# Output products in alternating row halves from one pool of six banks, turned weights for sixteen places at once, and softmaxes split into steps two pairs ahead

## The chip, the cores and the metric

One NeuronCore of a Trainium2 chip runs the whole program. The metric is the device time of one execution in microseconds (us); lower is better. The engines named below are PE (TensorE, matrix products), DVE (VectorE), ACT (ScalarE), POOL (GpSimd) and SP (SyncE, which issues the DMAs here). SBUF is the on-chip memory, PSUM the eight accumulator banks that PE writes and that DVE and ACT empty, HBM the memory outside.

## The reference

`x` is 8 x 2496 x 256, in fp32. Two Fourier transforms are followed by a soft mixture of experts with 32 slots:

```python
X = np.fft.fft(np.fft.fft(x, axis=1), axis=2).real      # 8 x 2496 x 256, seen as N x 256
logits = X @ phi                                        # N x 32
d = softmax(logits, over the N rows)                    # dispatch
slot_in = d.T @ X                                       # 32 x 256
slot_out = relu(slot_in @ w1[e]) @ w2[e]                # 8 experts, 4 slots each
c = softmax(logits, over the 32 slots)                  # combine
out = c @ slot_out                                      # N x 256
```

Every max is subtracted before its exponential and 1e-9 is added to each sum. The output is 20.45 MB of fp32.

## The kernel before, in words

The eight sequences are handled as four pairs p = 0 to 3. The table `ORDER` writes out the parts of the program in order, one letter for a part, one digit for the pair, one for a piece of it. A scheduler then puts the instructions of all parts into one queue for each engine; each engine runs its queue strictly in order, and `tc.issue_after(x)` keeps what it encloses behind the instruction x in that order.

**The first part** (parts a, z, t, b, c, e, d, u) loads x, folds and transforms it, makes logits (tile `lt`, kept for each pair), and accumulates the dispatch sums. It ends with the last sums of pair 3 (`u`, L376). **The middle** takes up about 20 us: `m` joins the pairs' sums (`accT`, `slotin`, and the slot inputs `sT`, L455 to L457), `l` is the first expert product (`h`, L475, then a ReLU on ACT into `hs`, L483, and a transpose on DVE into `hT`, L487), `v` the second (`so`, L495), and `r` replicates the slot outputs: `so` is copied to `sos` (L509 on ACT, L510 on DVE), multiplied with a selection matrix (`sorep`, L511), and scaled into the two halves of the operand `rh` (L512 on ACT, L513 on DVE).

**The softmax over slots** is part `s`, once for each pair: eleven transposes of `lt` into three PSUM banks (`cT`, L525), three copies on ACT into `c` (L530), and then, for each of two halves of 20 places, a max on DVE (L539), a subtraction on POOL (L540), the exponential on ACT (L541), a sum, an addition and a reciprocal on DVE (L542 to L544) and a multiplication on POOL (L545). Pairs 0 and 1 get theirs in the middle of the program, pairs 2 and 3 within the output stage; all stand behind the last `u` product.

**The output stage** is part `o`, for each pair five blocks b = 0 to 4 of eight places. For a block, PE transposes two 128-column pieces of `c` (`lT`, L555), ACT copies them to SBUF (`lTs`, L558), and four products `po` follow (L565), i = 0 to 3. Each product uses only 64 of the array's 128 rows: i = 0 and 2 use rows 0 to 63, i = 1 and 3 use rows 64 to 127 (`tile_position=(64 * (i % 2), 0)`). Each fills one PSUM bank (128 x 512). The even products take their bank from a pool of two (`ps`), the odd ones from a pool of three (`ps3`), and a seventh and eighth bank (`p1`) hold transposes. ACT copies the even products into the output tile `o` (128 x 2048, 1 MB), DVE the odd ones (L579). When a tile is full, SP issues its DMA to HBM (L586, and L584 for a 128 KB rest of each pair). The output tiles come from a ring of six buffers that x and the weights used before.

Every fp32 product appears in the trace as two records, each transpose as one.

Of the kernel before, what the change touches and what calls it, by code (L numbers as in the profile page):

```python
# [114 lines left out]
def _build(nc, tc, xh, phih, w1h, w2h, cins, where, out, out0):  # L115
# [4 lines left out]
    with ctx:  # L120
        cp = ctx.enter_context(tc.tile_pool(name="cp", bufs=1))
        sb = ctx.enter_context(tc.tile_pool(name="sb", bufs=1))
        pp = ctx.enter_context(tc.tile_pool(name="pp", bufs=P2, space=PSUM))
# [303 lines left out]
        def part_m():  # L427
# [21 lines left out]
            pe.matmul(ps[:1, 64:96], acc[:, 0:1], C("psum")[:, 0:32], start=True, stop=True)  # L449
            v.tensor_copy(at[:, :64], ps[:, :64])  # L450
            v.tensor_copy(at[:1, 32:64], ps[:1, 64:96])
            for lc in range(2):
                ps = bank3(f"slotin{lc}")
                ls = slice(lc * 128, lc * 128 + 128)
                pe.matmul(ps[:, :NSLOT], C("ta")[:, ls], at[:, 0:32], start=True, stop=False)  # L455
                pe.matmul(ps[:, :NSLOT], C("tb")[:, ls], at[:, 32:64], start=False, stop=True)
                (sc.copy, v.tensor_copy)[lc](sT[:, lc], ps[:, :NSLOT])  # L457
# [45 lines left out]
        def part_r():  # L503
# [5 lines left out]
            sc.copy(sos[:, :128], so[:, :128])  # L509
            v.tensor_copy(sos[:, 128:], so[:, 128:D])  # L510
            pe.matmul(ps[:, :D], C("sel2"), sos, start=True, stop=True)  # L511
            sc.activation(rh[0][:, 0], ps[:, :D], AF.Copy, scale=C("turn")[:, 0:1])  # L512
            v.tensor_scalar(rh[0][:, 1], ps[:, :D], C("turn")[:, 1:2], None, op0=ALU.mult)  # L513


        cq = {}

        def part_s(p):
            L = lt[p]
            cq[p] = sb.tile([128, 40, NSLOT], F32, name=f"c{p}", tag=CT[p], bufs=bufs_(CT[p]))  # L520
            for b in range(3):
                ps = bank1(f"cT{p}_{b}")
                n = min(4, NG - 4 * b)
                for j in range(n):
                    pe.transpose(  # L525
                        ps[:, 120 * j : 120 * j + 120],
                        L[:, 4 * b + j].rearrange("p s k -> p (s k)"), ident[:120, :120],
                    )
# [5 lines left out]
            e1 = nc.gpsimd if GP & 1 else v  # L534
            e2 = nc.gpsimd if GP & 2 else v
            for i in range(2):
                c = cq[p][:, 20 * i : 20 * i + 20]
                m = sb.tile([128, 2, 20], F32, name=f"cm{p}_{i}", tag="cm", bufs=2)
                v.tensor_reduce(m[:, 0], c, axis=AX.X, op=ALU.max)  # L539
                e1.tensor_tensor(c, c, m[:, 0].unsqueeze(2).to_broadcast([128, 20, NSLOT]), op=ALU.subtract)  # L540
                sc.activation(c, c, AF.Exp)  # L541
                v.tensor_reduce(m[:, 1], c, axis=AX.X, op=ALU.add)  # L542
                v.tensor_scalar(m[:, 1], m[:, 1], 1e-9, None, op0=ALU.add)
                v.reciprocal(m[:, 1], m[:, 1])  # L544
                e2.tensor_tensor(c, c, m[:, 1].unsqueeze(2).to_broadcast([128, 20, NSLOT]), op=ALU.mult)  # L545


        n_ev = [0]

        def part_o(p, b):  # L550
            ps = bank1(f"lT{p}_{b}")
            lT = et([128, 2, 128], f"lTs{p}_{b}")
            for t in range(2):
                k0 = 8 * b + 4 * t
                pe.transpose(  # L555
                    ps[:, t * 128 : t * 128 + 128], cq[p][:, k0 : k0 + 4].rearrange("p k s -> p (k s)"), ident
                )
            sc.copy(lT, ps[:, :256].rearrange("p (i n) -> p i n", i=2))  # L558
            ot = ring(f"o{p}_{b}")

            pos = []
            for i in range(4):
                pos.append((bank, bank3)[i % 2](f"po{p}_{b}_{i}"))
                rows = slice(64 * (i % 2), 64 * (i % 2) + 64)
                pe.matmul(  # L565
                    pos[i], lT[rows, i // 2], rh[0][rows].rearrange("p k d -> p (k d)"),
                    start=True, stop=True, tile_position=(64 * (i % 2), 0),
                )
                if i % 2 == 0:
                    continue  # L570
                part_ev(p, b, i - 1, pos[i - 1], ot)
                part_ev(p, b, i, pos[i], ot)

        done_ = {}

        def part_ev(p, b, i, po, ot):
            done = done_.get((p, b), 0)
            np_ = 64 if b == 4 and i == 3 else 128
            (v.tensor_copy if n_ev[0] % 2 else sc.copy)(  # L579
                ot[:np_, 2 * i : 2 * i + 2, :].rearrange("p k d -> p (k d)"), po[:np_]  # L580
            )
            n_ev[0] += 1
            if b == 4 and i == 3:
                nc.sync.dma_start(out0[p].rearrange("p (r d) -> p r d", d=D), ot[:64, 6:8])  # L584
            elif i == 3 or (b == 4 and i == 2) or ((p, b) == (0, 0) and i in FIRST):
                nc.sync.dma_start(  # L586
                    out[p, :, (8 * b + done) * D : (8 * b + 2 * i + 2) * D].rearrange("p (r d) -> p r d", d=D),
                    ot[:, done : 2 * i + 2],
                )
                done_[p, b] = 2 * i + 2  # L590
# [66 lines left out]
```

## Time and profile before

| | |
|---|---|
| time, median of 3 runs | 203.47 us (203.37 to 204.8) |
| the profiled execution: device time | 203.76 us |
| the profiled execution: span of the trace | 201.7 us |
| granted PE clock over the span | 0.982 |
| moved to and from HBM | 38.46 MB read, 20.45 MB written |

The device time of the profiled execution holds 2.06 us that lie outside the span. It is 0.29 us above the median. Times inside the trace count from the start of the span.

### The profile page before, as it was taken

How to read it: one execution, taken by the hardware profiler on the slowest of the kernel's cores; microseconds unless marked ns; L12 is line 12 of the kernel's file. 1: busy time of each engine (PE TensorE's matmuls, PEld its weight loads, DVE VectorE, ACT ScalarE, POOL GpSimd, SP SyncE). 2: the span in 40 equal slices, each digit the busy share in tenths (PEclk: the TensorE clock that was granted, in tenths of full speed). 3: DMA queues.
4: the chain of work that ended last, by engine and by line, in shares of the span. 5: the costliest groups of instructions: out<-in, count | busy, mean ns of one | idle time of the engine just before them, and what ended most of it. 6: DMA issues, size and time to landing. Idle time of an engine off the chain costs nothing.

```text
span 201.7 us, 4216 instructions
## 1 busy us (share of the span) xinstructions
PE 178.7 (89%) x1682; PEld 110.1 (55%) x1682; DVE 126.0 (62%) x228; ACT 111.9 (55%) x252; POOL 20.8 (10%) x25
## 2 busy tenths in 40 slices
PE   0489899899999899999989999997998999999930
PEld 0365586586778766568738772564443343334400
DVE  0599869999968926422575448634668458465600
ACT  2134686578872864757628355534657456556630
POOL 0000000000000000000000025730016225200000
PEclk9999999999999999999999999999999999999975
DMA  5999999999930998009506799801978588599996
GB/s 181 412 422 412 416 421 424 418 419 411 353 138 10 354 406 369 5 0 305 219 3 240 292 310 414 318 0 41 368 289 336 245 362 329 219 418 387 422 382 265
DMA packets 10706, 59.16 MB, mean 293 GB/s; under 512 B 1344, under 2 KB 1728, under 8 KB 5696
## 3 DMA queue, kind: packets, MB, share of 16 engines
q1 hardware_dynamic: 10688, 58.91, 73.9%
q8 instruction: 13, 0.21, 0.4%
q14 instruction: 5, 0.04, 0.0%
HBM read 38.46 MB, written 20.45 MB: 292 GB/s over the span
## 4 chain that ended last, share of the span: by engine, by line
PE 80%; DVE 6%; ACT 5%; DMA 2%; issue 1%; POOL 1%; SPq 0%; ACTq 0%; DVEq 0%
PE po L565 22%; PE pt L229 9%; PE z L244 8%; PE e L335 6%; PE d L353 5%; PE a L279 4%; PE u L376 4%; PE h L475 4%; PE so L495 3%; PE lT L555 3%; DMA x<-xh 2%; PE cT L525 2%; PE lp L297 2%; PE lm L298 2%; PE zt L265 2%; ACT et L230 2%
## 5 line engine op out<-in xcount | busy, mean ns | idle before, releaser
L565 PE MATMUL po<-rh,lTs 64*128 64x512 f32 x160 | 47.6, 617 | 1.7 <-DVE rh L513 1.1
L579 DVE COPY o<-po 128x512 f32<-128x512 f32 (+1 forms) x40 | 27.3, 686 | 14.8 <-PE po L565 14.6
L579 ACT COPY o<-po 128x512 f32<-128x512 f32 x40 | 23.4, 587 | 19.8 <-PE po L565 19.6
L229 PE MATMUL pt<-cs,eo 128*128 128x128 f32 x160 | 25.7, 294 | 8.2 <-DVE eo L224 7.9
L230 ACT COPY et<-pt 128x512 f32<-128x512 f32 x40 | 22.8, 587 | 14.3 <-PE pt L229 14.2
L565 PEld LDWEIGHTS po<-rh,lTs 64*128 64x128 f32 x160 | 17.9, 185 | 19.1 <-issue 8.8
L229 PEld LDWEIGHTS pt<-cs,eo 128*128 128x128 f32 x160 | 19.1, 149 | 14.8 <-DVE eo L224 7.9
L222 DVE TENSOR_TENSOR x<-x 128x1024 f32<-128x1024 f32 x16 | 19.4, 1215 | 3.2 <-DMA x<-xh 3.2
L244 PE MATMUL z<-et,wphi 128*32 128x256 f32 (+1 forms) x288 | 16.7, 368 | 2.3 <-ACT et L230 2.3
L540 POOL TENSOR_TENSOR c<-c,cm 128x640 f32<-128x640 f32 x8 | 10.0, 1265 | 74.8 <-DVE cm L539 73.6
L320 ACT ACTIVATE d<-lt,nm 120x128 f32<-120x128 f32 x44 | 13.7, 391 | 3.6 <-DVE nm L317 3.6
L335 PE MATMUL e<-cs,dpm 120*64 120x120 f32 x176 | 13.9, 273 | 0.0
L224 DVE TENSOR_TENSOR eo<-x 128x512 f32<-128x512 f32 x20 | 13.6, 682 | 0.3
L225 DVE TENSOR_TENSOR eo<-x 128x512 f32<-128x512 f32 x20 | 13.6, 680 | 0.0
L244 PEld LDWEIGHTS z<-et,wphi 128*32 128x32 f32 x288 | 8.1, 114 | 9.2 <-ACT et L230 3.8
L279 PE MATMUL a<-cs,zt 128*120 128x128 f32 x88 | 11.8, 279 | 1.0 <-DVE lt L302 0.9
L335 PEld LDWEIGHTS e<-cs,dpm 120*64 120x64 f32 x176 | 11.4, 136 | 2.4 <-issue 1.8
L252 ACT COPY zs<-z 128x512 f32<-128x512 f32 (+1 forms) x12 | 6.2, 513 | 10.4 <-PE z L244 10.4
L376 PE MATMUL u<-eo,ds 128*32 128x129 f32 x320 | 11.5, 275 | 0.1
L279 PEld LDWEIGHTS a<-cs,zt 128*120 128x120 f32 x88 | 10.4, 183 | 2.1 <-DVE lt L302 1.1
L353 PE MATMUL d<-e,cs 128*64 128x320 f32 x64 | 10.7, 443 | 0.5 <-ACT ds L359 0.5
L545 POOL TENSOR_TENSOR c<-c,cm 128x640 f32<-128x640 f32 x8 | 10.1, 1264 | 6.6 <-DVE cm L544 6.6
(94 smaller groups left out, 219.2 us busy)
## 6 DMA issues: line engine op xcount, KB each, us to landing
x<-xh SPq DMA_DIRECT2D x16, 1024.0 KB, 12.0
out<-o SPq DMA_DIRECT2D x15, 1024.0 KB, 4.3
w<-w1h SPq DMA_DIRECT2D x6, 1024.0 KB, 8.0
w<-w2h SPq DMA_DIRECT2D x12, 512.0 KB, 6.5
x<-xh SPq DMA_DIRECT2D x4, 896.0 KB, 12.4
out<-o SPq DMA_DIRECT2D x4, 768.0 KB, 4.3
w<-w1h SPq DMA_DIRECT2D x4, 512.0 KB, 5.5
w<-w2h SPq DMA_DIRECT2D x2, 1024.0 KB, 7.2
```

Source lines behind the costliest of these rows:

```text
L222: v.tensor_tensor(x[:, 0:4], x[:, 0:4], x[:, 4:8], op=ALU.add)
L224: v.tensor_tensor(e[:, :, 0:128], x[:, 0:4, 0:128], x[:, 0:4, 128:256], op=ALU.add)
L229: pe.transpose(b[:, g * 128 : g * 128 + 128], e[:, g, k * 128 : k * 128 + 128], ident)
L230: sc.copy(tr[k][:, :, :, qi, :], b.rearrange("p (g h a) -> p g h a", g=4, h=2))
L244: pe.matmul(z[32 * g : 32 * g + 32, o : o + n], wphi[:, w, :], tr[k][:, g].rearrange("p h q a -> p (h q a)"), start=w != 0, stop=w != 1, t ...
L279: pe.matmul(ps[:120, i * 128 : i * 128 + 128], zt[p][:, GS * g : GS * g + GS].rearrange("p s h c -> p (s h c)"), C("wa"), start=True, stop ...
L320: sc.activation(d[:, g], L[:, g], AF.Exp, bias=nm[:, g : g + 1], scale=1.0)
L335: pe.matmul(ps[64 * k : 64 * k + 64, 120 * i : 120 * i + 120], dpm[p, hf][:, k, 3 * j + i, :], C(name), start=True, stop=True, tile_positi ...
L353: pe.matmul(ps[64 * h : 64 * h + 64, :320], C("wb")[:, 64 * k : 64 * k + 64], esb[p].rearrange("p g (s h c) -> p (g s) h c", h=2, c=NKC)[: ...
L376: last = pe.matmul(ub[32 * g : 32 * g + 32, 0:129], dsb[p][:, k, c, :], e[:, 0:129] if k == 0 else e[:, 127:256], start=cc == 0, stop=cc == 9,
L565: pe.matmul(pos[i], lT[rows, i // 2], rh[0][rows].rearrange("p k d -> p (k d)"), start=True, stop=True, tile_position=(64 * (i % 2), 0),)
L579: (v.tensor_copy if n_ev[0] % 2 else sc.copy)(ot[:np_, 2 * i : 2 * i + 2, :].rearrange("p k d -> p (k d)"), po[:np_])
```

## The change

The products of a block are written in couples: two banks are taken from one pool `po` of six banks, product h = 0 (rows 0 to 63) and h = 1 (rows 64 to 127) are queued one behind the other, and each product is held behind the one before it. ACT empties h = 0, DVE h = 1. The six banks are those of the old pools `ps`, `ps3` and `u`, which are closed after part `r`.

The transposes of `c` move into a part of their own, `k`, with sixteen places at a time for j = 0 and 1 and eight for j = 2: four, four and two transposes, and one copy on ACT for each (128x512, 128x512, 128x256).

The softmaxes of pairs 2 and 3 become six steps, part `x`: transposes and copies; both maxima and subtractions; one exponential; the other; sum to multiplication of one half; of the other. `ORDER` puts the steps of pair 2 between the blocks of pair 0, and those of pair 3 between blocks of pairs 1 and 2. Parts `k` and `x` are held behind the latest product and the latest copies of `o`.

In the middle, the transposes of pairs 0 and 1 are held behind `u`, `accT` or `slotin` one by one (`GATE`), the rest of their softmaxes behind the copies of `sT`, and both of those copies are made by DVE. `sos` is one copy on ACT, and both halves of `rh` are made on ACT.

```diff
-    "u30 m00 l00 s00 l10 s10 v00 v10 r00 o00 o01 o02 o03 "
-    "o04 o10 s20 o11 o12 o13 o14 s30 o20 o21 o22 o23 "
+    "u30 m00 l00 s00 l10 s10 v00 v10 r00 k00 o00 k01 x20 o01 x21 o02 k02 x22 o03 "
+    "k10 x23 o04 x24 o10 k11 x25 o11 x30 o12 k12 x31 o13 k20 x32 o14 x33 o20 k21 "
...
+GATE = {0: ['u', 'acc', 'acc'], 1: ['slot', 'slot', 'slot']}
...
-                (sc.copy, v.tensor_copy)[lc](sT[:, lc], ps[:, :NSLOT])
+                anchor["sT"] = v.tensor_copy(sT[:, lc], ps[:, :NSLOT]).ins
...
-            sc.copy(sos[:, :128], so[:, :128])
-            v.tensor_copy(sos[:, 128:], so[:, 128:D])
+            sc.copy(sos, so[:, :D])
...
-            v.tensor_scalar(rh[0][:, 1], ps[:, :D], C("turn")[:, 1:2], None, op0=ALU.mult)
+            for k in range(2):
+                sc.activation(rh[0][:, k], ps[:, :D], AF.Copy, scale=C("turn")[:, k : k + 1])
+            banks.close()
+            pool_o.append(ctx.enter_context(tc.tile_pool(name="po", bufs=6, space=PSUM)))
...
+        def part_s(p):
+            logits(p)
+            with tc.issue_after(anchor["sT"]):
+                for i in range(2):
+                    less_max(p, i)
+                    exp(p, i)
+                    over_sum(p, i)
...
+            n = 4 if j < 2 else 2
+            lT = et([128, 4, 128], f"lTs{p}_{j}")
...
+            sc.copy(lT[:, :n], ps[:, : 128 * n].rearrange("p (i n) -> p i n", i=n))
...
+                po = [pool_o[0].tile([128, 512], F32, name=f"po{p}_{b}_{2 * t + h}", tag="po") for h in range(2)]
+                for h in range(2):
+                    rows = slice(64 * h, 64 * h + 64)
+                    with tc.issue_after(behind["pe"]) if "pe" in behind else nullcontext():
+                        ins = pe.matmul(
+                            po[h], lts[p, b, t][rows], rh[0][rows].rearrange("p k d -> p (k d)"),
+                            start=True, stop=True, tile_position=(64 * h, 0),
+                        )
+                    behind["pe"] = ins.ins
+                for h, ev in ((0, sc.copy), (1, v.tensor_copy)):
+                    i = 2 * t + h
...
+                    behind[h] = ins.ins
...
+                for ins in behind.values() if behind else [anchor["u"]]:
+                    order.enter_context(tc.issue_after(ins))
+                f(*a)
```

**PE, early in the output stage.** In these rows `po_2_1` is product i = 1 of block b = 2, the number behind it counts buffers; `lT` are transposes of `c`, `cT` those of the logits for a later softmax. Before, in pair 0:

```order
L565 MATMUL po_2_1_1723<-rh,lTs_2_1716 128x512
L565 MATMUL po_2_3_1729<-rh,lTs_2_1716 128x512
L565 MATMUL po_2_0_1721<-rh,lTs_2_1716 128x512
L565 MATMUL po_3_1_1742<-rh,lTs_3_1735 128x512
L565 MATMUL po_2_2_1727<-rh,lTs_2_1716 128x512
L525 MATMUL cT_0_1793<-cs_70,lt_942 128x120 x4
L565 MATMUL po_3_3_1748<-rh,lTs_3_1735 128x512
L565 MATMUL po_4_1_1761<-rh,lTs_4_1754 128x512
L565 MATMUL po_3_0_1740<-rh,lTs_3_1735 128x512
L565 MATMUL po_4_3_1767<-rh,lTs_4_1754 128x512
L565 MATMUL po_3_2_1746<-rh,lTs_3_1735 128x512
```

And now, from the second block of pair 0 on:

```order
L588 MATMUL lT_1_1702<-cs_70,c_1508 128x128 x4
L529 MATMUL cT_0_1710<-cs_70,lt_942 128x120 x4
L604 MATMUL po_1_0_1728<-rh,lTs_0_1680 128x512
L604 MATMUL po_1_1_1729<-rh,lTs_0_1680 128x512
L604 MATMUL po_1_2_1734<-rh,lTs_0_1680 128x512
L604 MATMUL po_1_3_1735<-rh,lTs_0_1680 128x512
L529 MATMUL cT_1_1716<-cs_70,lt_942 128x120 x4
L604 MATMUL po_2_0_1748<-rh,lTs_1_1703 128x512
L604 MATMUL po_2_1_1749<-rh,lTs_1_1703 128x512
L529 MATMUL cT_2_1722<-cs_70,lt_942 128x120 x3
L604 MATMUL po_2_2_1754<-rh,lTs_1_1703 128x512
L604 MATMUL po_2_3_1755<-rh,lTs_1_1703 128x512
```

Before, odd products ran ahead of the even ones of their block, so that products of one row half also stood behind each other; now even and odd alternate without exception, and the logits' transposes of pair 2 stand two blocks earlier.

**DVE at the same place.** Rows `o<-po` are copies of products, the `TENSOR_REDUCE` rows are maxima of pair 2's softmax. Before:

```order
L579 COPY o_2_1720<-po_2_1_1723 128x512
L579 COPY o_2_1720<-po_2_3_1729 128x512
L579 COPY o_3_1739<-po_3_1_1742 128x512
L579 COPY o_3_1739<-po_3_3_1748 128x512
L579 COPY o_4_1758<-po_4_1_1761 128x512
L579 COPY o_4_1758<-po_4_3_1767 64x512
L539 TENSOR_REDUCE cm_0_1810<-c_1792 128x20
```

And now:

```order
L612 COPY o_2_1747<-po_2_1_1749 128x512
L545 TENSOR_REDUCE cm_0_1741<-c_1709 128x20
L545 TENSOR_REDUCE cm_1_1744<-c_1709 128x20
L612 COPY o_2_1747<-po_2_3_1755 128x512
L612 COPY o_3_1767<-po_3_1_1769 128x512
L612 COPY o_3_1767<-po_3_3_1775 128x512
```

The maxima moved from behind pair 0's last block to between the two odd copies of its third.

**DVE in the middle.** `at` is the input of `slotin`, `sT` its copied result, `cm` the softmax of pair 0. Before:

```order
L451 COPY at<-accT 1x32
L539 TENSOR_REDUCE cm_0_1526<-c_1508 128x20
L539 TENSOR_REDUCE cm_1_1534<-c_1508 128x20
L457 COPY sT<-slotin_1473 128x32
L542 TENSOR_REDUCE cm_0_1526<-c_1508 128x20
```

And now:

```order
L452 COPY at<-accT 1x32
L459 COPY sT<-slotin_1469 128x32
L459 COPY sT<-slotin_1473 128x32
L545 TENSOR_REDUCE cm_0_1526<-c_1508 128x20
L545 TENSOR_REDUCE cm_1_1534<-c_1508 128x20
L553 TENSOR_REDUCE cm_0_1526<-c_1508 128x20
```

The copies of `sT` now stand ahead of the maxima of pair 0, and DVE makes both.

More of the change, by code (lines that the diff above doesn't have):

```diff
@@ L448, in part_m @@
             pe.matmul(ps[:, 0:64], acc[:, 1:129], C("psum"), start=True, stop=True)
[L449 removed]
+            ins = pe.matmul(ps[:1, 64:96], acc[:, 0:1], C("psum")[:, 0:32], start=True, stop=True)
+            anchor["acc"] = ins.ins
             v.tensor_copy(at[:, :64], ps[:, :64])
@@ L523, in part_s @@
                 n = min(4, NG - 4 * b)
[L524 to L528, printed above, removed]
+                with tc.issue_after(anchor[GATE[p][b]]) if p in GATE else nullcontext():
+                    for j in range(n):
+                        pe.transpose(
+                            ps[:, 120 * j : 120 * j + 120],
+                            L[:, 4 * b + j].rearrange("p s k -> p (s k)"), ident[:120, :120],
+                        )
                 w = min(GS * n, NSLOT - 12 * b)
@@ L533, in part_s @@
                 )
[L534 to L545, printed above, removed]
@@ L548, in _build, with half, less_max @@
[L548 to L554, printed above, removed]
+        def half(p, i):
+            return cq[p][:, 20 * i : 20 * i + 20]
+        def less_max(p, i):
+            cm[p, i] = sb.tile([128, 2, 20], F32, name=f"cm{p}_{i}", tag="cm", bufs=4)
+            c, m = half(p, i), cm[p, i][:, 0]
+            v.tensor_reduce(m, c, axis=AX.X, op=ALU.max)
+            nc.gpsimd.tensor_tensor(c, c, m.unsqueeze(2).to_broadcast([128, 20, NSLOT]), op=ALU.subtract)
@@ new lines, in part_x, with part_k @@
+        def part_x(p, step):
+            if step == 0:
+                logits(p)
+            elif step == 1:
+                less_max(p, 0)
+                less_max(p, 1)
+            elif step < 4:
+                exp(p, step - 2)
+            else:
+                over_sum(p, step - 4)
+        behind, lts = {}, {}
+        def part_k(p, j):
+            ps = bank1(f"lT{p}_{j}")
+            n = 4 if j < 2 else 2
+            lT = et([128, 4, 128], f"lTs{p}_{j}")
+            for t in range(n):
+                k0 = 16 * j + 4 * t
@@ L557, in part_o @@
                 )
-            sc.copy(lT, ps[:, :256].rearrange("p (i n) -> p i n", i=2))
+            sc.copy(lT[:, :n], ps[:, : 128 * n].rearrange("p (i n) -> p i n", i=n))
+            for t in range(n):
+                lts[p, 2 * j + t // 2, t % 2] = lT[:, t]
+        def part_o(p, b):
             ot = ring(f"o{p}_{b}")
[L561 to L590, printed above, removed]
@@ L599, in _build @@
+        def after(f, *a):
+            with ExitStack() as order:
+                for ins in behind.values() if behind else [anchor["u"]]:
+                    order.enter_context(tc.issue_after(ins))
+                f(*a)
         parts = {
```

46 lines of the change are left out of this document (31 added, 15 removed), and 2 rows, old and new, of the table ORDER.

## The prediction

> **What bounds the kernel now.** I read the page's head first, then the chain of work that ended last, then the DMA by windows.
>
> ```profile
> span 201.7 us, 4216 instructions
> PE 178.7 (89%) x1682; PEld 110.1 (55%) x1682; DVE 126.0 (62%) x228; ACT 111.9 (55%) x252; POOL 20.8 (10%) x25
> HBM read 38.46 MB, written 20.45 MB: 292 GB/s over the span
> PE 80%; DVE 6%; ACT 5%; DMA 2%; issue 1%; POOL 1%; SPq 0%; ACTq 0%; DVEq 0%
> ...
> 185.94 7.32 PE po L565 x26
> 193.28 0.59 ACT o L579
> ```
>
> By these rows PE carries the span: 89% busy, 80% of the chain. But the chain ends at 193.87 us (193.28 + 0.59), and the span is 201.7. The last 7.8 us hold no compute at all. What fills them stands in the windows, whose columns are stretch, length, busy time of PE, weight loads, DVE, ACT and POOL, clock, DMA share, GB/s:
>
> ```profile
> 139.78:175.00 35.22, 34.60 (x136) 14.94 (x133) 23.30 (x41) 20.61 (x43) 10.02 (x8) 1.00 0.74 295
> 176.00:194.00 18.00, 17.25 (x68) 7.02 (x68) 9.96 (x15) 11.26 (x23) 0.00 (x0) 1.00 1.01 415
> 140.00:141.00 1.00, 1.00 (x6) 0.58 (x6) 0.80 (x2) 0.90 (x3) 0.00 (x0) 1.00 0.37 139
> 199.50:200.00 0.50, 0.00 (x0) 0.00 (x0) 0.00 (x0) 0.00 (x0) 0.00 (x0) 0.50 0.69 283
> 200.00:201.70 1.70, 0.00 (x0) 0.00 (x0) 0.00 (x0) 0.00 (x0) 0.00 (x0) 0.50 0.01 4
> ```
>
> From 176 us on the DMA is saturated at 415 GB/s, and it stays so until about 199.95. It started at 140.63 (37% of the window 140 to 141). The output's 20.45 MB at 415 GB/s need **49.3 us**; the DMA took 59.3. So it waited for data for **10.0 us**, all before 176, where it ran at 295 GB/s. The stage has two limits in turn: first PE makes products too slowly for the DMA, then the DMA drains what has piled up. A faster PE is worth at most those 10.0 us, however much PE time it saves.
>
> The time is thus: start T0 of the first product, 2.62 us until its data move (140.63 - 138.01), 49.3 us, the DMA's idle time, 1.75 us to the end of the span (201.7 - 199.95), 2.06 us outside it (203.76 - 201.7). For before: 138.01 + 2.62 + 49.3 + 10.0 + 1.75 + 2.06 = 203.74. The profiled run lies 0.29 us above the median, which I take off at the end.
>
> **PE's part.** How long does a product take, alone and beside another?
>
> ```profile
> 138.01 3.78 PE L565 MATMUL po<-rh,lTs 64*128 64x512 f32 x16 [1.08 <-DVE rh L513]
> 139.17 0.59 ACT L579 COPY o<-po 128x512 f32<-128x512 f32 x1 [1.73 <-PE po L565]
> 139.21 0.69 DVE L579 COPY o<-po 128x512 f32<-128x512 f32 x1 [1.26 <-PE po L565]
> 140.02 0.59 ACT L579 COPY o<-po 128x512 f32<-128x512 f32 x1 [0.27 <-PE po L565]
> 141.72 0.44 PE L555 MATMUL lT<-cs,c 128*128 128x128 f32 x2
> 142.08 2.84 PE L565 MATMUL po<-rh,lTs 64*128 64x512 f32 x10
> 144.85 0.63 PE L525 MATMUL cT<-cs,lt 120*128 120x120 f32 x4
> 145.41 2.84 PE L565 MATMUL po<-rh,lTs 64*128 64x512 f32 x10
> 150.97 0.65 PE L555 MATMUL lT<-cs,c 128*128 128x128 f32 x4
> 151.55 1.12 PE L565 MATMUL po<-rh,lTs 64*128 64x512 f32 x2
> ```
>
> The first row is 8 products, in alternating halves. Both products of a couple are ready within 0.04 us (139.17 and 139.21), and the next couple 0.85 later: two products of different halves share one slot of **0.86 us**. The run at 142.08 is five products in the order odd, odd, even, odd, even: the first is alone, the others form two couples, three slots. It lasts 2.77 us to the next row, 3 x 0.86 and 0.19 for the turn to full-height transposes. Blocks of transposes cost 0.36 (two, 141.72 to 142.08), 0.58 (four `lT`, 150.97 to 151.55) and 0.56 (four `cT`, 144.85 to 145.41); three `cT` I take at 0.46, four less one transpose of 0.11 (from 0.58 - 0.36 for two).
>
> In the order before, the 80 products make 32 couples and 16 singles, 48 slots, among 18 blocks of transposes. Now they make 40 couples, 40 slots, among 14 blocks. Before: 48 x 0.86 = 41.3, 18 turns 3.4, transposes 8.3 (11 x 0.36, 2 x 0.58, 3 x 0.56, a block of seven 0.87, one of three 0.46), together 53.0; the remaining 2.9 us to 193.87 are waits and the last copy. Now: 40 x 0.86 = 34.4, 14 turns 2.7, transposes 8.4 (seven blocks of four `lT`, four of two, 22 `cT`, neighbours merged), together 45.5. **PE saves 7.5 us**, before waits.
>
> **What keeps up beside it.** The copies and the softmax, for this stage:
>
> ```profile
> L579 DVE COPY o<-po 128x512 f32<-128x512 f32 x36 | 24.6, 686 | 13.7 <-PE po L565 13.5
> L579 ACT COPY o<-po 128x512 f32<-128x512 f32 x40 | 23.4, 587 | 19.8 <-PE po L565 19.6
> L558 ACT COPY lTs<-lT 128x256 f32<-128x256 f32 x17 | 6.2, 376 | 1.1 <-PE lT L555 1.1
> L545 POOL TENSOR_TENSOR c<-c,cm 128x640 f32<-128x640 f32 x4 | 5.1, 1263 | 4.4 <-DVE cm L544 4.4
> L542 DVE TENSOR_REDUCE cm<-c 128x20 f32<-128x640 f32 x4 | 3.3, 820 | 1.1 <-ACT c L541 1.1
> L541 ACT ACTIVATE c<-c 128x640 f32<-128x640 f32 x4 | 3.0, 748 | 1.4 <-POOL c L540 1.4
> L544 DVE RECIPROCAL cm<-cm 128x20 f32<-128x20 f32 x4 | 1.1, 272 | 0.1
> L543 DVE TENSOR_SCALAR cm<-cm 128x20 f32<-128x20 f32 x4 | 0.8, 197 | 0.1
> ```
>
> Within a slot of 0.86 us ACT copies 0.59 and DVE 0.69, so a lone stream of couples leaves DVE 0.17. With six banks, three couples are in flight: 2.58 us, against some 1.9 from a product's start to its free bank (0.86 to its end, 0.30 until its copy starts, 0.69). The softmax has to fit besides. The first ten tiles now hold both softmaxes: 20 x 0.69 + 4 x 2.1 (two reduces of 0.82, small steps 0.20 and 0.27) = 22.2 us of DVE, while PE needs 24.1 (17.2 in slots, 6.9 in blocks and turns) and the DMA 24.6. No engine is over, but little is spare. Over all 80 products DVE has 40 x 0.69 + 4 x 2.1 = 36 us of work against the DMA's 49.3: if DVE alone set the pace of the copies, the sum below would stand. The Trainium skill (TensorEngine Tiling, PSUM Bottleneck) warns that tiling speeds up PE and not the emptying of PSUM, so that the copies may become the limit; no run here shows that yet, and by the two sums above it would not change the time unless the queue order makes the copies late, which is the third rival below.
>
> **The DMA's idle time now.** Tile (0,0) is gone at T0 + 5.1 (2.62 and 1 MB in 2.5). Tile (0,1)'s last product starts after three slots and the first block (two times four transposes and a turn, 1.2), at 3.8; with 1.16 to its copy, 0.69 for it and 0.9 from issue to moving data (139.78 in the row of SP's first issue below, to 140.63), its data move at 6.55: **1.4 us** idle. Tile (0,2): six couples, of which the sixth starts at 5 x 0.86 + 1.2 + 0.75 + 0.65 = 6.9 (two more blocks with turns). Its odd copy now stands behind two maxima on DVE, and those wait for the third copy of `cT`: product ends come to 145.2 + 1.16 by my T0, while the maxima run from 146.0 to 147.6 and the copy to 148.3. Data move at T0 + 10.9, the tile before was gone at 9.05: **1.8 us**. Following the queues further with these durations, PE waits 0.7 us for `lTs` copies that stand behind an exponential or copies on ACT, at the end of pair 0 and of pair 1 (near T0 + 11.6 and T0 + 26.5), and the DMA idles 0.3 before tiles (1,1) and (1,3). From then on tiles come every 2.1 to 2.2 us on average and leave every 2.5, so nothing more is lost: idle **3.8 us** instead of 10.0. The ring of six tiles is not reached: about three are waiting at the end.
>
> ```profile
> 139.78 6.17 SPq L586 DMA_DIRECT2D out<-o  x5
> ```
>
> The same 26 transfers go through SP, now in order of tiles, each rest of 128 KB behind its block instead of ahead; with one queue and a saturated DMA that moves nothing.
>
> **T0.** In the middle the order on DVE and ACT changes.
>
> ```profile
> 118.82 1.55 DVE L539 TENSOR_REDUCE cm<-c 128x20 f32<-128x640 f32 x2 [0.51 <-ACT c L530]
> 120.28 0.18 DVE L457 COPY sT<-slotin 128x32 f32<-128x32 f32 x1
> 122.24 0.74 ACT L541 ACTIVATE c<-c 128x640 f32<-128x640 f32 x1 [0.49 <-POOL c L540]
> 123.19 0.69 ACT L483 ACTIVATE hs<-h,sm 128x512 f32<-128x512 f32 x1 [0.20 <-PE h L475]
> 123.92 0.16 PEld L475 LDWEIGHTS h<-w,sT 128*32 128x32 f32 x8 [0.86 <-ACT hs L483]
> 135.32 0.27 ACT L509 COPY sos<-so 128x128 f32<-128x128 f32 x1 [1.41 <-PE so L495]
> 135.62 0.29 DVE L510 COPY sos<-so 128x128 f32<-128x128 f32 x1 [2.98 <-ACT sos L509]
> 136.33 0.60 PE L511 MATMUL sorep<-sos,cs 128*128 128x256 f32 x2
> ```
>
> `sT` moves ahead of the maxima on DVE, which saves little, since PE has transposes to fill that wait: `h` starts at 120.2 instead of 120.33. But the maxima start about 1 us later (119.8), so do the subtractions on POOL, and the second exponential, which stands ahead of `hs` on ACT, slips from 122.24 to about 123.3. `hs` then ends near 124.85 instead of 123.88, and PE, which waits for its bank in the fifth row, is held 0.95 us, for which three transposes of pair 1 are the only filler; their work merely moved. Behind it `so` ends 0.95 later, by the same work. Then the end gets shorter: one copy of 0.38 (the row of 128x256) replaces two that ran to 135.91, which gains 0.2; six transposes no longer stand between `sos` and `sorep` (136.33 - 135.91, less 0.1), 0.3; the second half of `rh` on ACT, 0.05. Net +0.4; bounds are -0.6, where the later softmax is hidden wholly, and +1.0, where a second `hs` slips as well. I take +0.3, near the waiting row: **T0 = 138.3**.
>
> **Sum.** 138.3 + 2.62 + 49.3 + 3.8 + 1.75 + 2.06 = 197.8; less 0.29: **197.5 us**, 6.0 less than 203.47 (2.9%).
>
> The Trainium skill (DMA: Bandwidth & Descriptors, Where 436 GB/s comes from) has transfers between HBM and SBUF bound at about 358 GB/s per core, by which the writes alone would take 57.1 us and the sum 205.3. The row at 176 us (415 GB/s over 18 us) speaks against it, and the fabric figure of 435 on that page fits it better.
>
> **Rivals.**
> 1. *The DMA is fed without a gap.* Idle falls to nothing if the early copies fit better than I follow them: T0 138.0 and no idle give 193.4. Against it: the two gaps above follow from blocks of transposes that PE must pass.
> 2. *The couples don't hold, or bring nothing.* If the second product of a couple often waits for DVE's later copy, couples fall apart and idle stays near 10: 203.5. For it: DVE's copy is 0.10 longer than ACT's. Against it: each half has its own 0.86 us period, and the first row shows four couples at full pace while both engines copy.
> 3. *The softmax steps stop the copies, and it gets slower.* On DVE each half's sum stands ahead of copies and waits for an exponential on ACT, which waits for POOL. One step fully exposed is 1.26 + 0.75 + 0.82 + 0.47 = 3.3 us, four are 13.2. PE would then end at T0 + 45.5 + 13.2 + 1.9 for the last copy, 198.9; with 0.9 and the last 0.9 MB (2.2 us) DMA ends at 202.0 and the time is 205.5. It decides from about 11 us of exposed waits. Against it: each sum stands at least three copies (2.1 us) behind its subtraction.
> 4. *Part of that*: waits of 4 to 6 us more than I count, or T0 at 139.0 with idle 6: 200.4.
>
> **Chances.** Forecast (195.6 to 199.2) 0.66; first rival (193.0 to 195.6) 0.14; fourth (199.2 to 201.4) 0.12; second 0.05; third 0.03. The range 194.0 to 200.2 takes the forecast, most of the first and half of the fourth, with the bounds of T0 and of the idle. About 1% (2 us) is what a measurement tells from no change: faster beyond it (below 201.4) 0.92, same 0.05, slower 0.03.
>
> **What would show it.** Couples: ACT and DVE copies start together every 0.86 us, and PE ends near 186 us instead of 193.9. DMA: idle near 141 to 150, saturated at about 415 GB/s from 160 on, 8 us or more of transfers after the last copy. T0: the first product at 138.3, with `h` waiting for `hs` near 124. Wrong I would be if DVE waited for `c` with full banks behind it, if writes ran below 400 GB/s, or if T0 moved by more than 1 us.

## The result

The changed kernel takes **198.87 us** (median of 6, 198.17 to 199.05) against 204.05 us for the kernel before, run beside it (6, 203.37 to 204.8): a ratio of 0.9742 [0.9712, 0.9771], 5.2 us less. The forecast was 197.5 us, range 194.0 to 200.2. The profiled execution took 199.02 us. Three kernels below (the rest queued first, the changed kernel with half the output, the old middle with halves everywhere) have no view here: their profiled execution was a slow one (566, 226 and 285 us), and their times are those of the other executions.

The head of the changed kernel's page, the shares of its chain, and the last piece of the chain:

```profile
span 196.9 us, 4194 instructions
PE 79%; DVE 6%; ACT 4%; DMA 2%; issue 2%; POOL 1%; SPq 0%; ACTq 0%; DVEq 0%
...
184.91 0.68 DVE o L612
```

The chain still says PE, and now it ends at 185.59 us, 8.3 us earlier than before. The span is only 4.8 us shorter: 11.3 us without any compute stand at its end, where there were 7.8. The windows of the changed kernel (stretch, length, busy time of PE, weight loads, DVE, ACT, POOL, clock, DMA share, GB/s):

```profile
140.00:150.00 10.00, 9.61 (x51) 4.48 (x51) 6.28 (x10) 6.94 (x14) 2.49 (x2) 1.00 0.65 265
150.00:193.00 43.00, 34.58 (x165) 14.99 (x161) 27.43 (x46) 25.62 (x47) 7.54 (x6) 0.97 1.01 407
193.00:194.00 1.00, 0.00 (x0) 0.00 (x0) 0.00 (x0) 0.00 (x0) 0.00 (x0) 0.50 0.68 244
194.00:195.00 1.00, 0.00 (x0) 0.00 (x0) 0.00 (x0) 0.00 (x0) 0.00 (x0) 0.50 0.27 82
195.00:196.00 1.00, 0.00 (x0) 0.00 (x0) 0.00 (x0) 0.00 (x0) 0.00 (x0) 0.50 0.03 10
```

And the end of the kernel before:

```profile
198.50:199.50 1.00, 0.00 (x0) 0.00 (x0) 0.00 (x0) 0.00 (x0) 0.00 (x0) 0.50 1.04 436
199.50:200.50 1.00, 0.00 (x0) 0.00 (x0) 0.00 (x0) 0.00 (x0) 0.00 (x0) 0.50 0.36 148
```

From 150 us on the DMA is saturated for 43 us without a pause; before, it reached that only at 176. So the transfers set the end. But the end looks different: before, the share falls from 1.04 to nothing within half a microsecond; now it runs out over more than two (0.68, 0.27, 0.03).

To compare the runs I cut every span in the same way. T0 is the first product; data move 2.62 us later, since from T0 to SP's first issue it is 1.77 us in the changed kernel and in the experiments read below (139.91 - 138.14 here). The 20.45 MB need 50.25 us at 407 GB/s. The **tail** is the end of the span less the moment at which the bytes left after the full-rate stretch would have been gone at 407 GB/s: here 0.336 MB after 193 make 193.83, so 196.9 - 193.83 = 3.1. What remains is **idle**: 193.83 - 140.76 - 50.25 = 2.8 (it takes in slower packets).

| kernel (one profile each) | T0 | idle | tail | span |
|---|---|---|---|---|
| before | 138.0 | 9.0 | 1.8 | 201.7 |
| changed | 138.1 | 2.8 | 3.1 | 196.9 |
| alternating alone | 137.9 | 3.0 | 2.3 | 196.1 |
| softmaxes late | 137.6 | 5.5 | 2.2 | 198.2 |
| four tiles | 138.2 | 2.7 | 2.7 | 196.5 |
| old middle | 136.4 | 2.8 | 3.4 | 195.5 |
| 512 KB everywhere | 137.9 | 2.9 | 1.9 | 195.5 |
| 512 KB, first pair | 138.2 | 2.4 | 2.3 | 195.8 |
| 512 KB, last pair | 137.9 | 3.1 | 2.8 | 196.7 |
| old middle, 512 KB in first pair | 136.7 | 2.4 | 2.2 | 194.2 |

T0 itself carries scatter from the first part, which no edit touches. In the chains, the last group of `u` starts between 113.61 and 114.80 us in these profiles:

```profile
114.14 2.39 PE u L376 x76
114.70 2.39 PE u L376 x76
113.61 2.39 PE u L376 x76
```

These are the kernel before, the changed kernel and the old middle. A difference of T0 is read below from this group on.

The couples are there. Copies of the changed kernel on ACT and DVE, and PE's products as a group:

```profile
142.21 0.58 ACT L612 COPY o<-po 128x512 f32<-128x512 f32 x1 [0.42 <-PE po L604]
143.07 0.59 ACT L612 COPY o<-po 128x512 f32<-128x512 f32 x1 [0.27 <-PE po L604]
...
142.26 0.69 DVE L612 COPY o<-po 128x512 f32<-128x512 f32 x1 [1.37 <-PE po L604]
143.12 0.69 DVE L612 COPY o<-po 128x512 f32<-128x512 f32 x1 [0.17 <-PE po L604]
...
145.71 1.55 DVE L545 TENSOR_REDUCE cm<-c 128x20 f32<-128x640 f32 x2 [0.28 <-ACT c L534]
147.17 2.06 DVE L612 COPY o<-po 128x512 f32<-128x512 f32 x3
...
149.44 2.85 PE L604 MATMUL po<-rh,lTs 64*128 64x512 f32 x12 [0.39 <-ACT lTs L591]
```

Both copies of a couple start 0.05 us apart, the next couple 0.86 later. The two maxima stand in front of three copies as followed by hand, and PE waits 0.39 us for `lTs` at 149.44, which is T0 + 11.3.

### The profile page after: what moved, and what is told of

Same layout as the page of the kernel before. It is cut to its first block, busy times and chain, and to the rows that moved or that the text cites. A ratio compares the mean times of both kernels' runs of the same rounds, so it can differ in the third digit from the quotient of the medians.

```text
span 196.9 us, 4194 instructions
## 1 busy us (share of the span) xinstructions
PE 170.5 (87%) x1682; PEld 106.8 (54%) x1682; DVE 125.4 (64%) x227; ACT 111.2 (56%) x244; POOL 20.8 (11%) x25
## 3 DMA queue, kind: packets, MB, share of 16 engines
HBM read 38.46 MB, written 20.45 MB: 299 GB/s over the span
## 4 chain that ended last, share of the span: by engine, by line
PE 79%; DVE 6%; ACT 4%; DMA 2%; issue 2%; POOL 1%; SPq 0%; ACTq 0%; DVEq 0%
PE po L604 18%; PE pt L229 10%; PE z L244 8%; PE e L335 6%; PE d L353 5%; PE a L279 5%; PE u L376 4%; PE h L477 4%; PE so L497 4%; PE cT L529 3%; PE lp L297 2%; DMA x<-xh 2%; PE lT L588 2%; PE lm L298 2%; PE zt L265 2%; ACT et L230 2%
## 5 line engine op out<-in xcount | busy, mean ns | idle before, releaser
L604 PE MATMUL po<-rh,lTs 64*128 64x512 f32 x160 | 38.7, 610 | 1.6 <-ACT rh L514 0.9
L229 PE MATMUL pt<-cs,eo 128*128 128x128 f32 x160 | 26.2, 301 | 7.7 <-DVE eo L224 7.6
L229 PEld LDWEIGHTS pt<-cs,eo 128*128 128x128 f32 x160 | 19.8, 153 | 14.2 <-DVE eo L224 7.6
L604 PEld LDWEIGHTS po<-rh,lTs 64*128 64x128 f32 x160 | 14.2, 186 | 16.4 <-issue 11.3
```

The costliest lines, as they stand in the source:

```text
L229: pe.transpose(b[:, g * 128 : g * 128 + 128], e[:, g, k * 128 : k * 128 + 128], ident)
L604: ins = pe.matmul(po[h], lts[p, b, t][rows], rh[0][rows].rearrange("p k d -> p (k d)"), start=True, stop=True, tile_position=(64 * h, 0),)
```

## The experiments

### Which part of the change carries it

**Alternating alone.** The kernel before, with each product held behind the one before it, and nothing else:

```diff
+                with tc.issue_after(last_[0]) if last_ else nullcontext():
-                pe.matmul(
+                    ins = pe.matmul(
                     pos[i], lT[rows, i // 2], rh[0][rows].rearrange("p k d -> p (k d)"),
                     ...
+                last_[:] = [ins.ins]
```

> The kernel before with one thing added: each output product is held behind the one before it in program order, so the two row halves alternate; pools, transposes, softmaxes and the middle stay as before. Theory (the gain is PE slots: 48 become 40, and the DMA is fed earlier): the first product stays at 138.0 us, PE ends near 186.5 instead of 193.9, the DMA idles about 5 us instead of 10, time about 200 us, that is 4 us less than before and 1 us more than the full change. Rival (the six banks and the softmax steps carry the gain, alternation by itself is stopped by waits for banks): idle stays at 8 us or more, time 202 to 204.

Measured: **198.75 us** (197.91 to 199.25), ratio 0.973 [0.9686, 0.9774]. That is the time of the whole change, and less than the theory's 200 us: the idle time fell to 3.0 us, not to 5. Its chain ends, and its windows run:

```profile
178.14 7.36 PE po L567 x32
...
185.52 0.68 DVE o L582
...
140.00:152.00 12.00, 12.00 (x60) 5.18 (x57) 8.49 (x13) 9.11 (x19) 2.49 (x2) 1.00 0.94 382
152.00:156.00 4.00, 3.60 (x18) 1.88 (x18) 3.78 (x8) 3.27 (x8) 2.18 (x2) 1.00 0.38 138
156.00:193.00 37.00, 29.05 (x131) 12.06 (x127) 22.68 (x36) 20.11 (x41) 5.36 (x5) 0.93 1.00 407
193.00:194.00 1.00, 0.00 (x0) 0.00 (x0) 0.00 (x0) 0.00 (x0) 0.00 (x0) 0.50 0.83 262
194.00:195.00 1.00, 0.00 (x0) 0.00 (x0) 0.00 (x0) 0.00 (x0) 0.00 (x0) 0.50 0.15 53
```

PE's last product ends at 185.50: from T0 47.6 us, against 55.3 before (193.28 - 138.01) and 46.8 in the changed kernel (184.89 - 138.14). The order of the products gives 7.6 us of PE's time, all other edits together 0.9. The idle time is nearly the same in sum, at another place: DVE has the softmax of pair 2 in its queue and starts no copy between 150.72 and 153.10, and the transfers run short in one stretch (152 to 156), where the changed kernel loses some between 140 and 150.

**The softmax steps.** The changed kernel with the softmaxes of pairs 2 and 3 whole, at their places of before:

```diff
-... k00 o00 k01 x20 o01 x21 o02 k02 x22 o03 k10 x23 o04 x24 o10 k11 x25 o11 x30 o12 ...
+... k00 o00 k01 o01 o02 k02 o03 k10 o04 o10 s20 k11 o11 o12 k12 o13 k20 o14 s30 o20 ...
```

> The full change, but the softmaxes of pairs 2 and 3 each in one piece at their old places (behind the transposes of pair 1 and behind its last block). Theory (steps two pairs ahead keep the softmax out of the way of the copies): PE stops for about 4 us more in all at the starts of pairs 2 and 3, the DMA idles about 4 us more, time 202 to 203. Rival (the place of the softmax does not matter because the DMA has a backlog by then): no more than 0.5 us above the full change, 198.9 to 199.4.

Measured: **201.52 us** (200.2 to 202.69), ratio 0.9868 [0.9809, 0.9927]. That lies between the theory and its rival. In this form the steps are worth 2.7 us by the medians. The profiled execution is the fastest of the four (200.2 us): its idle time is 2.7 us longer than the changed kernel's, but T0 and the tail are 0.5 and 0.9 us shorter. DVE's rows and the windows of this kernel show the third rival's mechanism:

```profile
152.49 1.50 DVE L610 COPY o<-po 128x512 f32<-128x512 f32 x2 [1.39 <-PE po L602]
...
157.23 0.82 DVE L551 TENSOR_REDUCE cm<-c 128x20 f32<-128x640 f32 x1 [1.42 <-ACT c L547]
159.19 0.68 DVE L610 COPY o<-po 128x512 f32<-128x512 f32 x1
...
171.31 0.82 DVE L551 TENSOR_REDUCE cm<-c 128x20 f32<-128x640 f32 x1 [1.42 <-ACT c L547]
...
156.00:164.00 8.00, 7.19 (x31) 2.80 (x29) 5.79 (x12) 5.26 (x10) 4.17 (x4) 1.00 0.66 276
172.00:176.00 4.00, 3.17 (x10) 1.20 (x10) 3.98 (x11) 2.77 (x6) 2.01 (x2) 1.00 0.67 276
```

DVE stands 1.42 us for an exponential, twice, with copies behind it; no copy starts on DVE between 153.99 (the end of the pair at 152.49) and 159.19, and the DMA runs at two thirds. It is not the whole case for steps, though: alternating alone keeps the softmaxes whole as well and is 2.8 us faster. There, nothing holds the softmax behind products and copies, and the middle is the old one; which of these makes the difference was not tried by itself.

**The middle.** The changed kernel with the middle of before: no `GATE`, `sT`, `sos` and `rh` split between ACT and DVE again, no hold behind `sT`.

```diff
-GATE = {0: ['u', 'acc', 'acc'], 1: ['slot', 'slot', 'slot']}
+GATE = {}
-                anchor["sT"] = v.tensor_copy(sT[:, lc], ps[:, :NSLOT]).ins
+                (sc.copy, v.tensor_copy)[lc](sT[:, lc], ps[:, :NSLOT])
-            sc.copy(sos, so[:, :D])
+            sc.copy(sos[:, :128], so[:, :128])
+            v.tensor_copy(sos[:, 128:], so[:, 128:D])
...
+            v.tensor_scalar(rh[0][:, 1], ps[:, :D], C("turn")[:, 1:2], None, op0=ALU.mult)
```

> The full change in the output stage, with the middle of before: no gates on the transposes, slot inputs copied by ACT and DVE, the copies of the slot outputs and the two halves of the scaled operand split between ACT and DVE. Theory (the middle pays about as much as it gains): first product within 0.5 us of 138.1, time within 0.6 us of the full change, 198.3 to 199.5. Rival (the later softmax costs the 0.9 us that PE waits for the ReLU, and the shorter end gains less): first product near 137.4, time 198.1. Rival on the other side (the shorter end is what counts): first product near 138.8, time 199.6.

Measured: **197.62 us** (197.27 to 198.6), ratio 0.9686 [0.9643, 0.973], 1.25 less than the changed kernel and below all three expectations, as its first product at 136.43 us is. First the chain of the changed kernel from `h` on, with the weight load that was forecast to wait:

```profile
120.68 3.57 PE h L477 x32
124.25 0.46 PE cT L529 x3
...
124.75 3.64 PE h L477 x32
128.38 0.59 PE lT L588 x4
128.97 7.09 PE so L497 x128
...
124.74 0.16 PEld L477 LDWEIGHTS h<-w,sT 128*32 128x32 f32 x8 [0.26 <-ACT hs L485]
```

Then, from the chain with the old middle:

```profile
119.87 5.45 PE h L477 x48
...
128.13 5.85 PE so L497 x105
```

From the start of `h` to the end of `so` it is 15.38 us in the first and 14.11 in the second: `h` held for `hs` (0.50, filled with three `cT`) and four `lT` ahead of `so` (0.59) are gone from the path. The `lT` follow `so` here, while the copies of `sos` run. From there to the first product the old split takes 2.45 us (136.43 - 133.98), the new one 2.08. From `h` on the new middle thus loses 0.9 us. Ahead of `h` it gains 0.28: from the last group of `u` to `h` it takes 5.98 us (114.70 to 120.68), with the old middle 6.26 (113.61 to 119.87), and in the kernel before 6.27 (114.14 to 120.41). In all, the new middle costs 0.62 us (23.44 against 22.82 from that group to the first product); the other 1.09 us of T0's difference is the first part. So only half of the 1.25 us between the medians is traced to the middle, and whether the rest is chance isn't shown. Which hold brings which cost or gain wasn't tried apart.

### What the saved time on PE is worth without the DMA

Both kernels without the transfers of blocks 1 and 3 of each pair:

```diff
+                    elif b in (1, 3):
+                        pass
```

> The kernel before without the transfers of blocks 1 and 3 of each pair: 8 of the 20 MB of output are never written, all arithmetic stays. With 12.4 MB (30 us at 415 GB/s) the transfers can't be the limit behind the first product, and the end shows what TensorE and the copies need. Theory (in the kernel before, TensorE ended at 193.9 us of its own accord and the transfers only 6 us behind it): the last copy stays at 193 to 194 us, the last transfer lands some 3.3 us later, 199.5 to 200.8 us in all. Rival (TensorE was itself held by full output tiles, so that its end was that of the transfers): the last copy comes before 191 us, and the time is under 198.

> The changed kernel without the transfers of blocks 1 and 3 of each pair (8 of the 20 MB of output are never written, all arithmetic stays). Theory: the last copy stays at 185 to 186 us, the last transfer lands 3 to 4 us later, 191.5 to 193 us in all, about 8 us under the kernel before in the same form: that is what the change saves on TensorE and the copies, of which the transfers let only 5.2 us through. Rival (part of the 8 us is from transfers that keep the copies or the products waiting): the two kernels in this form differ by under 6 us.

Measured: **200.72 us** (199.98 to 200.93) for the kernel before and **192.33 us** (191.52 to 192.59) for the changed one, 8.4 us apart. With the full output it is 5.2. In this form the kernel before has its first product, and the end of its chain, at

```profile
138.89 1.56 PE L565 MATMUL po<-rh,lTs 64*128 64x512 f32 x6 [1.08 <-DVE rh L513]
...
186.84 7.32 PE po L565 x26
...
194.18 0.59 ACT o L579
```

Its first product is 0.88 us later than with all transfers (138.89 for 138.01), through the first part, and its last copy 0.90 later (194.18 for 193.28). From the one to the other nothing changed: no transfer had held PE there. So the change saves some 8.4 us on the way through PE and the copies, and 3.2 of them end in front of a DMA that is already full.

### The end of the transfers

**The order of the last two transfers.** In the last block of each pair the 128 KB rest was queued ahead of the 768 KB:

```diff
                     if b == 4 and i == 3:
                         nc.sync.dma_start(out0[p].rearrange("p (r d) -> p r d", d=D), ot[:64, 6:8])
+                        nc.sync.dma_start(
+                            out[p, :, 8 * b * D : (8 * b + 6) * D].rearrange("p (r d) -> p r d", d=D), ot[:, 0:6],
+                        )
-                    elif i == 3 or (b == 4 and i == 2) or ((p, b) == (0, 0) and i in FIRST):
+                    elif (i == 3 and b < 4) or ((p, b) == (0, 0) and i in FIRST):
```

> The changed kernel with the transfers of each pair's last block the other way round: the 128 KB of its lower rows (2 KB to a packet) are queued first and the 768 KB behind them, so that the last transfer of the run has packets of 12 KB. In the changed kernel the transfers were at full rate to 193 us and then thinned out over two microseconds (0.72, 0.65, 0.37 and 0.17 of the engines in the half microseconds from 193.0), where before the end was sharp. Theory 1, the sixteen engines drift apart during 40 us of unbroken work, and the slower ones end later: the tail of two microseconds stays, 198.5 to 199.2 us. Theory 2, the small packets at the very end make the tail: it goes, and the time falls by 0.9 to 1.4 us to 197.5 to 198.0 us.

(768 KB over 128 rows are 6 KB a row, not 12.) Measured: **198.3 us** (197.8 to 198.5), ratio 0.9708 [0.9675, 0.9742]: between the two theories, and within the uncertainty of the changed kernel. By itself it is inconclusive. The first two experiments say more: they queue the small rest last, too, and their tails are 2.3 and 2.2 us, not 3.1. So a small rest at the end doesn't by itself make the long tail; what the order is worth (0.57 us by the medians) isn't settled.

**Four tiles in the ring.**

```diff
         def part_o(p, b):
+            if (5 * p + b) % 4 == 0 and p + b > 0:
+                ring(f"skip{p}_{b}"), ring(f"skop{p}_{b}")
             ot = ring(f"o{p}_{b}")
```

> The changed kernel with four output tiles in turn instead of six (two of each six are taken and left unused), so that at most some 4 MB of output wait in the queue and the copies are held by transfers. In the changed kernel the last copy ended at 185.6 us and the transfers at 195.4, so 10 us of work, about 4 MB, were queued at the end. Theory 1 in its narrower form, the engines drift apart the more, the deeper the queue in front of them is: the tail of the transfers is shorter than two microseconds, and the time falls by up to 1 us, to 197.8 to 198.6. Theory 1 in its wider form (drift with unbroken work, at any depth) and theory 2 (small packets at the end): the last copies come 2 to 5 us later and the end does not move, 198.5 to 199.2 us. If holding the copies starves the transfers somewhere, it is slower than 199.5.

Measured: **199.04 us** (198.59 to 200.13), ratio 0.9757 [0.9719, 0.9796]. The experiment missed its aim. The last copy starts at 185.00 us against 184.91, so four tiles hold nothing back, and the queue was as deep as in the changed kernel. The tail of 2.7 us tells nothing of depth.

**Transfers of 512 KB**, one behind each couple: everywhere, in the first pair alone, in the last pair alone.

```diff
-                    elif i == 3 or (b == 4 and i == 2) or ((p, b) == (0, 0) and i in FIRST):
+                    elif i in (1, 3) or (b == 4 and i == 2) or ((p, b) == (0, 0) and i in FIRST):
```

```diff
+                    elif i == 3 or (i == 1 and p == 0) or (b == 4 and i == 2) or ((p, b) == (0, 0) and i in FIRST):
```

> The full change, with a transfer for each couple of products (512 KB, 4 KB per row) instead of one for each tile (1 MB, 8 KB per row). Theory (the early gaps wait for whole tiles; the end is ragged because the 16 DMA engines drift apart in a long unbroken queue): data flow earlier, the idle time falls by 0.5 to 1 us, the ragged end stays, time 198.0 to 198.6. Rival (19 more transfers cost issue time and shorter packets): time 199.5 or more.

> The changed kernel with 512 KB transfers in the first pair alone, 1 MB after it. It separates the two gains of the halves. If they come from the start (transfers begin a couple earlier while TensorE still sets the pace, idle time 2.9 to 1.4 us) the time falls by 1.0 to 1.5 us to 197.4 to 197.9, and the two microseconds of thinning transfers at the end stay. If they come from the end, it stays at 198.5 to 199.1 us.

> The changed kernel with 512 KB transfers in the last pair alone, whose 5 MB are the last to be written. If the thinning of two microseconds at the end comes from the size of the last transfers (large packets end far apart), it goes and the time falls by 1 to 1.5 us to 197.4 to 197.9. If it is built up over the 43 us in which the transfers never pause (sixteen engines that drift apart), the last 5 MB change little: the tail stays over 1.5 us and the time at 198.4 to 199.1.

Measured: everywhere **197.54 us** (197.24 to 198.56), ratio 0.9691 [0.9642, 0.974]; first pair **197.47 us** (196.56 to 198.46), 0.9676 [0.9646, 0.9705]; last pair **198.66 us** (198.03 to 199.16), 0.973 [0.9703, 0.9757]. The gain of 1.4 us comes with the first pair, by its time as expected; the last pair has none. The windows, everywhere first:

```profile
140.00:150.00 10.00, 9.61 (x49) 4.42 (x49) 6.11 (x9) 7.10 (x14) 2.49 (x2) 1.00 0.82 326
150.00:193.00 43.00, 34.30 (x163) 14.82 (x159) 27.43 (x46) 25.37 (x47) 7.55 (x6) 0.95 1.01 395
193.00:194.00 1.00, 0.00 (x0) 0.00 (x0) 0.00 (x0) 0.00 (x0) 0.00 (x0) 0.50 0.77 242
194.00:195.00 1.00, 0.00 (x0) 0.00 (x0) 0.00 (x0) 0.00 (x0) 0.00 (x0) 0.50 0.02 8
```

In the first pair alone:

```profile
140.00:150.00 10.00, 9.61 (x49) 4.45 (x49) 6.35 (x10) 6.88 (x14) 2.49 (x2) 1.00 0.78 312
163.00:164.00 1.00, 0.74 (x6) 0.05 (x2) 0.83 (x2) 1.00 (x3) 0.88 (x1) 1.00 0.61 254
193.00:194.00 1.00, 0.00 (x0) 0.00 (x0) 0.00 (x0) 0.00 (x0) 0.00 (x0) 0.50 0.58 174
194.00:195.00 1.00, 0.00 (x0) 0.00 (x0) 0.00 (x0) 0.00 (x0) 0.00 (x0) 0.50 0.09 35
```

In the last pair alone:

```profile
193.00:194.00 1.00, 0.00 (x0) 0.00 (x0) 0.00 (x0) 0.00 (x0) 0.00 (x0) 0.50 0.87 256
194.00:195.00 1.00, 0.00 (x0) 0.00 (x0) 0.00 (x0) 0.00 (x0) 0.00 (x0) 0.50 0.31 82
```

The early gain is there: 326 and 312 GB/s between 140 and 150 in place of 265, so 0.6 and 0.5 MB more by 150 us. But the halves everywhere run at 395 instead of 407 GB/s, which gives 0.5 MB back by 193 us. In the profiles a good part of the gain lies in the tail (1.9 and 2.3 for 3.1 us), which I had not expected of the first pair: with it the transfers pause again at 163 (share 0.61), where the changed kernel runs on (share 1.10 and 0.94 in the two halves of that microsecond). In the last pair the same pieces leave a tail of 2.8.

Taken together: the tail is 2.7 to 3.4 us in the four kernels whose transfers ran the last 43 us unbroken, in pieces of 1 MB for all but the last pair. It is 1.8 to 2.3 in those that paused later (kernel before, alternating alone, softmaxes late, first pair, and with 2.2 the kernel of the next section) and 1.9 with small pieces all through.

The trace also records every packet of a transfer, with its start, length and size but not its engine. The last packet ends 1.4 us before the end of the span in both kernels (200.28 of 201.7 before, 195.49 of 196.9 now), so the longer tail lies ahead of it. Before, the sixteen packets of 4 bytes that close the last transfer end within 0.55 us of each other (199.73 to 200.28). In the changed kernel the 64 packets of the last 128 KB rest, of 0.08 to 0.15 us each, are spread over 2.87 us (192.62 to 195.49). So the tail is one of engines that end apart.

That they drift apart as long as work never runs out (theory 1) isn't shown. For it: the packets of the four pairs' rests are spread over 1.2, 2.0, 2.8 and 2.9 us in the changed kernel and 1.3, 2.5, 2.6 and 3.2 with the old middle, against 0.9, 1.0, 0.8 and 1.3 in the kernel before. Against a plain growth since the last pause: with 512 KB in the first pair it is 2.5 us at 168, five microseconds behind the pause, and then 2.1 and 2.0. No run inserted a pause and nothing else, and each tail is from one profile.

### Both gains together

The old middle, with 512 KB everywhere and in the first pair alone (edits as above):

> The changed kernel with both edits that made it faster: the middle of the kernel before (h not held for hs, sT and the two stages behind so split between ScalarE and VectorE) and a transfer of 512 KB behind every couple of products. With the old middle alone the first product came 1.7 us earlier (136.43 against 138.14 us) and the transfers idled 2.6 us on their way to full rate at 148 us; with the halves alone that idle time fell from 2.9 to 1.35 us and the tail at the end from 2 to 0.5 us, while the packets of the 20 MB took 52.3 engine-us in place of 50.9. Theory, the two add: 197.62 less 1.0 to 1.9, so 195.7 to 196.6 us. Rival, both remove the same idle time of the transfers: 197.2 to 197.6 us, no better than either.

> The changed kernel with the middle of the kernel before and 512 KB transfers in the first pair alone, 1 MB after it: the two edits that gained, without the smaller packets where they bring nothing (52.3 against 51.1 engine-us with the halves everywhere and in the first pair alone). Theory, a first product about 1 us earlier and transfers that idle 1.2 us less are two separate terms of one sum: 198.87 less 1.25 less 1.4, so 196.0 to 196.5 us. Rival, with an earlier first product the transfers catch up with TensorE again and idle as much more: 196.9 to 197.5 us, where the two edits with halves everywhere came out (197.16 us).

Measured: everywhere **197.16 us** (196.61 to 197.44), ratio 0.9661 [0.9635, 0.9687], which is the rival's value: 0.4 us less than either edit alone. In the first pair alone **196.48 us** (196.02 to 196.73), ratio 0.9637 [0.9617, 0.9656], at the upper end of what the sum of the two terms gave. Its first product and its windows:

```profile
136.72 1.99 PE po L604 x8
...
139.00:148.00 9.00, 8.63 (x44) 3.78 (x42) 5.98 (x9) 6.09 (x13) 2.48 (x2) 1.00 0.82 325
161.50:162.00 0.50, 0.50 (x4) 0.00 (x0) 0.50 (x1) 0.50 (x2) 0.50 (x1) 1.00 0.02 0
148.00:191.00 43.00, 35.13 (x165) 15.32 (x165) 27.41 (x46) 26.20 (x48) 7.54 (x6) 0.95 0.99 399
191.00:192.00 1.00, 0.00 (x0) 0.00 (x0) 0.00 (x0) 0.00 (x0) 0.00 (x0) 0.50 0.88 307
192.00:193.00 1.00, 0.00 (x0) 0.00 (x0) 0.00 (x0) 0.00 (x0) 0.00 (x0) 0.50 0.29 88
```

T0 is 1.4 us, idle 0.4 and tail 0.8 below the changed kernel's; of T0, 0.6 us is the middle and 0.8 again the first part (its last group of `u` starts at 113.89). With the first pair's smaller pieces the transfers stand still once more, at 161.5 to 162, and the short tail comes back with it, as it did with the pause at 163 above. It is the fastest kernel here, 3.6% below the kernel before; its interval doesn't touch that of the changed kernel. Why the halves everywhere lose 0.7 us against it is open without a view of that kernel; the slower packets seen above (395 GB/s) are a possible cause.

## Why the prediction was right, and where it was off

- **The bound** was read rightly. The end is that of the transfers: 8.4 us of work saved, 5.2 us of time. The time came out 1.4 us above the forecast, inside its range.
- **PE's sum** of 45.5 us and 0.7 of waits stands against 46.8 measured, with the two forecast waits for `lTs` at 149.44 (0.39 us) and 163.90 (0.26 us, T0 + 25.8). Alternating alone gained 7.6 us: 6.9 by the slots (8 x 0.86) and 0.6 by three turns, since its products run past 15 blocks of transposes where there were 18. So the slots were the right unit. In the sum for the kernel before, the transposes come to 8.1 us by their own terms, not 8.3; the saving would then be 7.3, against 8.5 measured from T0 to the last product.
- **T0** was 138.14 for 138.3, in part by luck. From the last group of `u` on, the first product came after 23.87 us before (114.14 to 138.01) and after 23.44 now (114.70 to 138.14): the middle got 0.43 us shorter, where 0.3 longer was forecast, and a first part that ended 0.56 later hid it. `h` waited for `hs`, as said, and the shorter end made up for it. What the forecast undersized is the gain ahead of `h` (0.29 us, for 0.13 from 120.33 to 120.2), and what it left unseen is that the hold and the four `lT` cost about a microsecond that needn't be spent.
- **Idle time and rate** belong together, and their errors cancel. The rate was taken as 415 GB/s from 18 us of the kernel before; over 43 us it was 407, so the bytes need 50.25 us for 49.3, and idle is 2.8 for 3.8. From the first data to the moment when the bytes would be gone it is 53.1 us, as forecast (49.3 + 3.8). The gaps are where they were followed: by the packet records the second tile's data move at 144.70, T0 + 6.56 (forecast 6.55), the third's at 148.74, T0 + 10.60 (10.9); the two gaps of 0.3 behind them didn't come. Part of the lower rate lies in the 128 KB rests: while that of pair 0 is written (155.5 to 156.5) the transfers move 242 and 184 GB/s at a share of 0.95 and 1.02, and three rests lie in the 43 us, one in the 18. The Trainium skill (DMA: Bandwidth & Descriptors, Where 436 GB/s comes from) bounds transfers between HBM and SBUF at about 358 GB/s; the longer row contradicts that as the shorter one did.
- **The end of the transfers** is the term that was mis-sized: 1.75 us was copied from the kernel before, and it was 3.1 by the cut used here (1.8 before). These 1.3 us are nearly the whole miss; less 0.2 of T0, and 0.2 more for the time outside the span and the distance of the profile from the median.
- **The rivals**: no full feeding (idle 2.8), no broken couples (0.86 us apart), no stopped copies, and neither a T0 of 139 nor an idle time of 6. The third rival's wait is real, though: it appears as soon as the softmaxes are whole and late (1.42 us on DVE, twice; 2.7 us in time).

## What to carry to other kernels

When an engine feeds a queue of transfers, cut the span at the transfers: start, bytes at the rate of a long stretch, idle, tail; time saved upstream counts only as far as idle time is left. Try the smallest part of a change alone: the order of the products, one constraint, had the whole gain here, and among the edits beside it one, the middle, cost time. Small first pieces and large later ones gave the fastest kernel here; that is worth a try where a queue waits at its start. Before a gain or a loss is put down to an edit, take the scatter of an untouched part off: here it was up to 1.2 us.

## What the runs showed of the hardware

- Two fp32 products of 512 columns on opposite halves of PE's rows are ready for their copies within 0.05 us of each other, every 0.86 us, when they are queued alternately; that order alone took 7.6 us off PE's 55.3 from the first to the last product.
- After 43 us of unbroken writing in pieces of 1 MB the transfers ran out over more than two microseconds (share 0.68, 0.27, 0.03), against half a microsecond in the kernel before. The Trainium skill (DMA: Bandwidth & Descriptors, Why a DMA increments its semaphore by 16 and not by 1) says that the engines of one transfer finish independently, which agrees with such an end; the packet records here don't name the engine.
- Writes of 512 KB pieces ran at 395 GB/s, of 1 MB pieces at 407, each over the same 43 us. While a rest of 128 KB in rows of 2 KB was written, the rate fell to 242 and 184 GB/s in two half microseconds, with the transfers busy all the time.
